# Reordering the last two heads of a decode attention kernel, and filling TensorE's idle times in its tail with unread matmuls

## The chip, the cores and the metric

The kernel runs on one core of a Trainium2 chip. The metric is the device time of one execution in microseconds (us). The span, which the profile and every timed run list beside it, goes from the first to the last instruction; it is mostly 1.8 us shorter than the time. All runs told of here are "fast", which means that none is over 1.5% above the fastest run of the same kernel.

## The reference, cut to what matters

Four sequences decode one token each. The sum of three terms is returned: the input, attention over the last 2048 positions of a cache with 32 heads of 192, and a gated feed-forward block.

```python
xn = _layernorm(x)
q = (xn @ wq)                                   # 4 x 32 heads x 192
k = k_cache[:, :, Sk - W:, :]                   # W = 2048 of 8192 positions
v = v_cache[:, :, Sk - W:, :]
p = _softmax(einsum("bhqd,bhkd->bhqk", q, k) * Dh ** -0.5)
o = einsum("bhqk,bhkd->bhqd", p, v)
return x + o.reshape(B, 1, Hq * Dh) @ wo + (silu(xn @ w1) * (xn @ w3)) @ w2
```

## The kernel before: the parts that matter here

Each head's k block and v block are 3 MB loads. VectorE multiplies k with q in four quarters (`mult`), TensorE sums the products in six matmuls per quarter with an identity as weights (`adder`), VectorE finishes the sums (`reduce_quarter`). Then comes a chain across engines: maximum, transpose, broadcast of the maximum, exponent, and the masked weights `z`. TensorE multiplies them with v (`pv`), a copy and two f32 matmuls add the parts (`ge_sum`), VectorE scales and transposes a group of four heads (`ge_turn`), and TensorE projects it with a block of wo (`ge_proj`). `ffn_out` is the feed-forward block's last projection with w2.

Each engine works through its instructions in the order in which these functions are called. The order comes from a table of slots and phases; the parts for the tail are these:

```python
def pv(h):
    o_ps, z, vt = o_banks[h % 2], zs.pop(h), vts.pop(h)
    for jj in range(NJ // 2):                                  # 32 matmuls of 384 columns
        ...
    nc.scalar.copy(out=o_sb[:], in_=o_ps[:])

ends = {H - 2: (NU - 1, NU), H - 1: (NU + 3, NU + 4)}          # NU = 128 quarters
for h in range(H):
    u0, ul = h * GQ, h * GQ + GQ - 1
    ...
    for u in range(u0, ul + 1):
        add(u, 1, mult, u)
        add(u + 1, 2, adder, u)
        add(u + 1, 8, reduce_quarter, u)
    add(ul + 1, 9, chain_lmax, h)
    add(ul + 2, 3, chain_tr, h)
    add(ul + 2, 4, chain_gmax, h)
    add(ul + 3, 3, chain_bc, h)
    add(ul + 3, 4, chain_z, h)
    add(ul + 4, 5, ge_tot, h)
    ...
    v, m = ends.get(h, (u0 + L, u0 + L + 1))
    add(v, 7, pv, h)
    add(m, 7, ge_sum, h)
...
for h in range(H - 2, H):                                      # all loads of the tail, in this order
    add(NU - 6, 0, load_v, h)
add(NU - 6, 0, w2_load, 0)
add(NU - 6, 0, w2_load, 1)
add(NU - 6, 0, wo_load, NG - 2)
add(NU - 6, 0, wo_load, NG - 1)                                # the last wo block, 983 KB
add(NU - 6, 0, w2_load, 2)
add(NU - 6, 0, w2_load, 3)
add(e - 1, 8, ffn_out, 0)
add(e - 1, 8, ffn_out, 1)
add(e - 1, 8, ge_proj, NG - 2, 0, RPP)
add(e, 6, ge_proj, NG - 1, 0, RPP)                             # the last wo projection
add(e, 7, ffn_out, 2)                                          # with the next line: the last eight matmuls
add(e, 7, ffn_out, 3)
```

## Time and profile before

| | before |
|---|---|
| time, median of three runs | 526.53 us (526.12 to 526.58) |
| profiled span | 523.8 us |
| TensorE busy / VectorE busy | 69% / 65% |
| read from memory | 222.96 MB |

First the page of the kernel before: its rows over 40 equal slices of the span. PE is TensorE, PEld its weight loads, DVE VectorE, ACT ScalarE and POOL GpSimd. PEclk is the granted TensorE clock in tenths, DMA the busy share of the 16 DMA engines in tenths, GB/s what they moved.

```profile
PEclk9979886898878998789997988889878898889988
DMA  9999999999999999999999999999999999999996
GB/s 389 422 443 425 433 431 432 428 433 432 430 435 428 437 418 446 424 437 426 434 434 429 432 434 429 435 427 435 425 437 434 427 437 431 430 434 425 441 418 275
```

The loads never pause until the last slice; the kernel is bound by them, and only the tail behind them is open to this change. The chain that ended last, from its last long waits on, in columns of start, duration and what it was:

```profile
489.68 30.66 DMA w<-in_B_w_dram
520.34 0.04 issue
520.38 0.76 PE acc L264 x8
521.13 0.47 DVE res L542
```

The last w2 load lands at 520.34 us, and only the last eight matmuls, a cast and the output write follow. How close compute was to that shows in the timeline of TensorE in before's tail, with VectorE's transpose of head 31's group (start, duration, engine and line, what it did, and in brackets the idle time ahead of it and what ended it; L340 is `pv`, L264 the projections, L369 the transpose):

```profile
513.30 2.71 PE L340 MATMUL o_ps<-vt,z 128*8 128x384 bf16 x32 [0.24 <-DVE z L332]
...
518.65 0.38 DVE L369 STREAM_TRANSPOSE oT<-og 128x192 bf16<-128x192 bf16 x1
...
519.21 0.98 PE L264 MATMUL acc<-wo_t,oT 128*4 128x320 bf16 x12 [0.47 <-DMA wo_t<-in_A_wo_dram]
...
520.38 0.71 PE L264 MATMUL acc<-w,hT 128*4 128x320 bf16 x8 [0.19 <-DMA w<-in_B_w_dram]
```

Head 31's value product took 2.71 us, mostly at half clock (0.50 from 514 to 516 us). Its transposed output was ready at 519.03 us, 0.2 us ahead of the last wo projection, which waited for its load. The last eight matmuls waited for w2 as well. From the start of that wo projection to the start of the last eight it was 1.17 us; this distance does not shift with the loads.

The stretches of before's tail (the stretch, its length, busy us and instructions of each engine, then the granted clock, the DMA share and GB/s):

```profile
core 0: us, PE busy (x) PEld busy (x) DVE busy (x) ACT busy (x) POOL busy (x), PEclk, DMA share, GB/s
497.00:518.00 21.00, 16.38 (x130) 5.30 (x111) 11.68 (x16) 2.77 (x10) 0.00 (x0) 0.84 0.99 420
518.00:520.30 2.30, 1.72 (x25) 0.87 (x19) 0.80 (x2) 0.00 (x0) 0.00 (x0) 1.00 0.64 256
```

### The profile page before, as it was taken

The numbers are of one execution on the slowest core, as the hardware profiler recorded it, in microseconds if no ns is written. First come the engines' busy times: TensorE is split into PE (matmuls) and PEld (weight loads), VectorE is DVE, ScalarE is ACT, GpSimd is POOL, SyncE is SP. The second block draws the span as 40 slices with busy tenths as digits, with TensorE's granted clock in tenths as the row PEclk, the third lists the DMA queues.
The fourth block names the chain that finished last, engine by engine and source line by source line (L and its number), as shares of the span: only waits on it lengthen the run. The fifth ranks groups of instructions, "written<-read, shape, count | busy, mean of one in ns | idle before, by whom it ended". The sixth has DMA issues, their size and how long they took to land.

```text
span 523.8 us, 4820 instructions
## 1 busy us (share of the span) xinstructions
PE 361.8 (69%) x2336; PEld 75.9 (14%) x1643; DVE 340.9 (65%) x413; ACT 55.8 (11%) x176; POOL 5.6 (1%) x12
## 2 busy tenths in 40 slices
PE   0965866887668776667547768586686876675685
PEld 0100111121111111111111111111111111111122
DVE  3268853687656767577646877466667766667671
ACT  2111111111001110101100111001101110011111
POOL 4000000000000000000000000000000000000000
PEclk9979886898878998789997988889878898889988
DMA  9999999999999999999999999999999999999996
GB/s 389 422 443 425 433 431 432 428 433 432 430 435 428 437 418 446 424 437 426 434 434 429 432 434 429 435 427 435 425 437 434 427 437 431 430 434 425 441 418 275
DMA packets 11904, 223.26 MB, mean 426 GB/s; under 512 B 1332, under 2 KB 1608, under 8 KB 3052
## 3 DMA queue, kind: packets, MB, share of 16 engines
q1 hardware_dynamic: 11868, 222.96, 99.2%
q8 instruction: 15, 0.25, 0.2%
q14 instruction: 5, 0.04, 0.0%
q10 hardware_dynamic: 16, 0.01, 0.0%
HBM read 222.96 MB, written 0.01 MB: 426 GB/s over the span
## 4 chain that ended last, share of the span: by engine, by line
DMA 60%; PE 20%; DVE 15%; ACT 3%; issue 1%; SPq 1%
DMA kt<-in_A_k_cache_dram 44%; PE ps L288 11%; DMA w<-in_B_w_dram 11%; DVE pr L277 10%; DMA vt<-in_A_v_cache_dram 5%; PE po L361 4%; PE qps L243 3%; DVE sc L296 2%; ACT ex L324 1%; DVE z L332 1%; DMA x_sb<-in_A_x_dram 1%; PE mt L318 1%; ACT L324 0%; ACT negm L321 0%; PE mt L305 0%
## 5 line engine op out<-in xcount | busy, mean ns | idle before, releaser
L288 PE MATMUL ps<-pr,idb 128*128 128x512 bf16 x768 | 214.7, 422 | 137.6 <-DVE pr L277 137.5
L277 DVE TENSOR_TENSOR pr<-kt,qbc 128x3072 bf16<-128x3072 bf16 x128 | 223.5, 1746 | 104.0 <-DMA kt<-in_A_k_cache_dram 104.0
L296 DVE TENSOR_REDUCE sc<-ps 128x16 f32<-128x512 f32 x128 | 87.1, 681 | 2.7 <-PE ps L288 2.6
L340 PE MATMUL o_ps<-vt,z 128*8 128x384 bf16 x1024 | 60.5, 380 | 0.2 <-DVE z L332 0.2
L361 PE MATMUL po<-o_sb,sel_w 128*32 128x192 f32 x128 | 49.2, 518 | 0.6 <-ACT o_sb L343 0.6
L340 PEld LDWEIGHTS <-z 128*8 128x8 bf16 x1024 | 26.2, 95 | 98.8 <-issue 89.2
L332 DVE TENSOR_TENSOR z<-ex,mask_b 128x256 bf16<-128x256 bf16 x32 | 13.5, 423 | 38.6 <-ACT ex L324 38.6
L343 ACT COPY o_sb<-o_ps 128x384 f32<-128x384 f32 x32 | 15.3, 478 | 196.9 <-PE o_ps L340 196.9
L313 ACT ACTIVATE gneg<-gmax 1x128 f32<-1x128 f32 x32 | 9.8, 308 | 162.8 <-DVE gmax L310 162.8
L305 PEld LDWEIGHTS mt<-idf,lmax 128*1 128x1 f32 x32 | 3.2, 101 | 127.5 <-issue 125.5
L361 PEld LDWEIGHTS po<-o_sb,sel_w 128*32 128x32 f32 x128 | 13.8, 130 | 29.4 <-issue 27.9
L288 PEld LDWEIGHTS <-idb 128*128 128x128 bf16 x124 | 12.0, 97 | 39.3 <-issue 32.8
L318 PEld LDWEIGHTS mt<-ones_ff,gneg 1*128 1x128 f32 x64 | 9.6, 186 | 47.1 <-issue 43.7
L243 PE MATMUL qps<-wt,xnT 128*128 128x512 bf16 x59 | 14.9, 412 | 0.1
L318 PE MATMUL mt<-ones_ff,gneg 1*128 1x1 f32 x64 | 12.3, 259 | 0.7 <-ACT gneg L313 0.7
L321 ACT COPY negm<-mt 128x1 f32<-128x1 f32 x32 | 5.1, 159 | 70.4 <-PE mt L318 70.4
L310 DVE TENSOR_REDUCE gmax<-mt 1x4 f32<-1x128 f32 x32 | 8.8, 274 | 5.8 <-PE mt L305 5.8
L348 PEld LDWEIGHTS po<-rsum,tot_w 128*32 128x32 f32 x64 | 4.4, 108 | 51.5 <-ACT ex L324 35.4
L249 DVE CAST qbc<-qps 128x512 bf16<-128x512 f32 x6 | 3.8, 684 | 11.7 <-PE qps L243 11.7
L324 ACT ACTIVATE ex<-sc,negm 128x64 bf16<-128x64 f32 x32 | 11.1, 348 | 1.0
L305 PE MATMUL mt<-idf,lmax 128*1 128x128 f32 x32 | 10.9, 340 | 0.0
L199 PE MATMUL xnT_ps<-idb,xn 4*128 4x4 bf16 x5 | 0.4, 178 | 13.4 <-DVE xn L194 13.4
(74 smaller groups left out, 84.4 us busy)
## 6 DMA issues: line engine op xcount, KB each, us to landing
kt<-in_A_k_cache_dram SPq DMA_DIRECT2D x32, 3072.0 KB, 19.1
vt<-in_A_v_cache_dram SPq DMA_DIRECT2D x32, 3072.0 KB, 25.5
wo_t<-in_A_wo_dram SPq DMA_DIRECT2D x8, 960.0 KB, 20.7
wt<-in_A_wq_dram SPq DMA_DIRECT2D x2, 3072.0 KB
w<-in_B_w_dram SPq DMA_DIRECT2D x1, 1920.0 KB
wt<-in_A_wq_dram SPq DMA_DIRECT2D x1, 1536.0 KB, 19.5
w<-in_B_w_dram SPq DMA_DIRECT2D x1, 1536.0 KB
w<-in_B_w_dram SPq DMA_DIRECT2D x2, 640.0 KB
```

What stands on the lines that cost most here:

```text
L243: nc.tensor.matmul(qp[:], lhsT=xnT[:, kc].rearrange("p a b -> p (a b)"), rhs=wq_rows[kc][:, (c0 + i) * QC:(c0 + i + 1) * QC], start=(kc == ...
L277: nc.vector.tensor_tensor(out=pr[:], in0=kts[h][:, g * JQ:(g + 1) * JQ, :], in1=qbc[:, h * Dh:(h + 1) * Dh].unsqueeze(1).to_broadcast([P, ...
L288: nc.tensor.matmul(ps[:], lhsT=idb[:], rhs=pr[:, :, kk * DD:(kk + 1) * DD], start=(kk == 0), stop=(kk == NK - 1))
L296: nc.vector.tensor_reduce(out=scs[h][:, g * JQ:(g + 1) * JQ], in_=pss.pop(u)[:], axis=AX.X, op=ALU.add)
L305: nc.tensor.transpose(out=mt[0:1, 0:P], in_=chs[h][0][:], identity=idf[:])
L313: nc.scalar.activation(out=gneg[:], in_=gmax[:].unsqueeze(1).to_broadcast([1, PB, B]), func=ACTF.Copy, scale=-SCALE)
L318: nc.tensor.matmul(mt[:, P:P + 1], lhsT=gneg[:].rearrange("o p b -> o (p b)"), rhs=ones_ff[:], start=True, stop=True)
L324: nc.scalar.activation(out=ex[:], in_=scs.pop(h)[:], func=ACTF.Exp, bias=negm[:, 0:1], scale=SCALE, accum_out=rsum[:])
L332: nc.vector.tensor_tensor(out=z[:], in0=ex[:].unsqueeze(2).to_broadcast([P, NJ, B]), in1=mask_b[:].unsqueeze(1).to_broadcast([P, NJ, B]), ...
L340: nc.tensor.matmul(o_ps[c * CT:c * CT + 2 * B, :], lhsT=z[:, 2 * jj:2 * jj + 2, :], rhs=vt[:, 2 * jj:2 * jj + 2, :], start=(jj < 4), stop= ...
L343: nc.scalar.copy(out=o_sb[:], in_=o_ps[:])
L361: nc.tensor.matmul(po[sl, 0:Dh], lhsT=sel_w[:, par].rearrange("p a b -> p (a b)"), rhs=o_sb[:, par * Dh:(par + 1) * Dh].rearrange("p (r i) ...
```

## The change

The intent is to shorten the tail behind the last k block. Head 31's last two quarters are multiplied and summed ahead of head 30's value product, so that head 31's softmax can run while head 30's product is done. And 31 matmuls whose result nobody reads are put where TensorE was idle: 16 while the last k block is awaited, 3 and 6 in head 31's softmax chain, 3 ahead of the last wo projection, and 3 behind it. Busy time is meant to keep the clock from being halved. The first part of `ffn_out` also moves ahead of head 31's f32 sum. No load moves.

```diff
+    def warm(n):
+        if "warm" not in ffn:
+            ffn["warm"] = ps_t.tile([P, QC], FP32, tag="t", name="warm")
+        for _ in range(n):
+            nc.tensor.matmul(ffn["warm"][:], lhsT=idb[:], rhs=qbc[:, 0:QC], start=True, stop=True)
+
+    lastu = {NU - 2: (NU - 2, 1, NU - 2, 5), NU - 1: (NU - 2, 2, NU - 2, 6)}
-    ends = {H - 2: (NU - 1, NU), H - 1: (NU + 3, NU + 4)}
+    ends = {H - 2: (NU - 1, NU - 0.4), H - 1: (NU, NU + 1)}
 ...
-            add(u, 1, mult, u)
-            add(u + 1, 2, adder, u)
-            add(u + 1, 8, reduce_quarter, u)
-        add(ul + 1, 9, chain_lmax, h)
 ...
+            ms, mp, as_, ap = lastu.get(u, (u, 1, u + 1, 2))
+            add(ms, mp, mult, u)
+            add(as_, ap, adder, u)
+            add(min(u + 1, NU - 1), 8 if u != NU - 3 else 3, reduce_quarter, u)
+        a, b, c, d = (ul + 1, ul + 2, ul + 3, ul + 4) if h < H - 1 else (NU - 1, NU - 0.5, NU - 0.2, NU)
+        add(a, 9, chain_lmax, h)
 ...
+    add(NU - 3, 1.5, warm, 16)
+    add(NU - 0.3, 0, warm, 3)
+    add(NU - 0.1, 0, warm, 6)
 ...
-    add(e - 1, 8, ffn_out, 0)
+    add(e - 1, 5, ffn_out, 0)
     add(e - 1, 8, ffn_out, 1)
     add(e - 1, 8, ge_proj, NG - 2, 0, RPP)
+    add(e - 1, 9, warm, 3)
     add(e, 6, ge_proj, NG - 1, 0, RPP)
+    add(e, 7, warm, 3)
     add(e, 7, ffn_out, 2)
     add(e, 7, ffn_out, 3)
```

More of the change, by code (lines that the diff above doesn't have):

```diff
@@ L486 @@
         for u in range(u0, ul + 1):
-            add(u, 1, mult, u)
-            add(u + 1, 2, adder, u)
-            add(u + 1, 8, reduce_quarter, u)
-        add(ul + 1, 9, chain_lmax, h)
-        add(ul + 2, 3, chain_tr, h)
-        add(ul + 2, 4, chain_gmax, h)
-        add(ul + 3, 3, chain_bc, h)
-        add(ul + 3, 4, chain_z, h)
-        add(ul + 4, 5, ge_tot, h)
+            ms, mp, as_, ap = lastu.get(u, (u, 1, u + 1, 2))
[4 more added lines that the diff above has]
+        add(a, 9, chain_lmax, h)
+        add(b, 3, chain_tr, h)
+        add(b, 4, chain_gmax, h)
+        add(c, 3, chain_bc, h)
+        add(c, 4, chain_z, h)
+        add(d, 5, ge_tot, h)
         if h % HG == HG - 1:
-            add(ul + 4, 9, ge_rec, h // HG)
+            add(d, 9, ge_rec, h // HG)
         v, m = ends.get(h, (u0 + L, u0 + L + 1))
```

## The prediction

> **What bounds the kernel now.** The loads. The page's DMA row reads 9 in every slice but the last, at 430 GB/s or so. Of the 222.96 MB read, the stretch table gives 432 GB/s from 20 to 497 us and 420 GB/s from 497 to 518 us. The Trainium skill, "DMA: Bandwidth & Descriptors", section "Where 436 GB/s comes from", puts a ceiling at 435 GB/s; this trace sits just under it. TensorE (69% busy) and VectorE (65%) have slack. The chain of waits ends with loads: v until 489.7, then the w2 load until 520.34, then 0.76 us of the last projection's matmuls, 0.47 us of a cast, and the output write to 523.8.
>
> **What the tail looks like.** All loads of the tail are issued by 497.3 us, in an order the change leaves alone. The last k block lands at 497.0. The queue engine's closing waits put the landings of the two wo loads at 516.9 and 519.1 and w2's end at about 520.3. Compute is barely behind: head 31's value product ran 513.30 to 516.01 (2.71 us instead of 1.47, with a granted clock of 0.5 from 514 to 516), its transposed output was ready at 519.03, the last wo projection waited for its load and began at 519.21, ended 520.19, idled 0.19 us for w2, and the last eight matmuls ran 520.38 to 521.09.
>
> **What the change does.** It removes no work. Head 31's last two multiplies (1.75 us each) and sums go ahead of head 30's softmax product; head 31's chain no longer queues behind head 30's value product. It adds 31 unread 512-column matmuls (213 ns each at full clock, estimated from the six-matmul groups' 1.46 us; 6.6 us in all), 28 of them in idle TensorE time, which should hold the clock at 1.0. The Trainium skill, "TensorE: Matmul & The Clock Gate", Part 1, says that an idle window of about 3.4 us halves the clock; this trace agrees (idle 495.2 to 498.8, clock 0.5 from 500).
>
> **What that is worth.** Head 31's product can then start when its v block lands, about 511.5 us (estimate: landing order and 430 GB/s), take 1.5 us, and its transposed output be ready at about 516.5 instead of 519.0. That gain of 2.5 us is off the critical path: the last wo projection still waits for its load at 519.1, and the end for w2 at 520.3. Only about 0.1 us of before's tail waits for compute. Against that, the last three unread matmuls stand between the last wo projection (streaming done at about 520.05) and w2's final matmuls: 0.64 us, of which 0.3 us fits into the wait, so about 0.3 us is lost. In executions where the clock phase left before's end cold, the change could save up to 1 us (20 half-speed 320-column matmuls, in pairs, estimate). These nearly cancel.
>
> **Prediction: 526.5 us, 8 in 10 between 525.5 and 527.2.** Chances: faster by over 2%: 0.01; within 2%: 0.98; slower by over 2%: 0.01.
>
> **What would show it right.** Loads land at the same times after (last w2 at 520.3 within 0.5 us); the granted clock is near 1.0 from 499 to the end; head 31's product starts at v's landing, and its transposed output is ready 2 to 3 us earlier; the last wo projection still starts at its load's landing; no gap for w2 before the last eight matmuls, which start at about 520.7 behind the three unread ones.
>
> **What would make it wrong.** The loads themselves ending earlier or later (contention of TensorE's reads with writes to SBUF); before's unprofiled executions having a cold end, which makes the change about 1 us faster; the 16 unread matmuls running at half clock and pushing head 31's chain past its v block.

## The result, and the profile after

| | before | after |
|---|---|---|
| median of six runs each | 526.33 us (525.66 to 527.12) | 526.79 us (526.04 to 528.43) |
| profiled span | 523.8 us | 524.4 us |
| last wo projection starts | 519.21 us | 519.31 us |
| last eight matmuls start | 520.38 us | 520.98 us |

The ratio is 1.0015, with a 95% interval of 0.9994 to 1.0037: the same within 2%, and not clear of 1. A ratio is the mean time of one kernel's fast runs over that of the other's fast runs of the same rounds, so it is not quite the ratio of the medians.

The same rows of the page, after:

```profile
PEclk9979887989898999798897988789987899889999
DMA  9999999999999999999999999999999999999996
GB/s 387 424 433 428 440 428 428 433 431 431 427 441 429 429 423 443 426 441 427 426 439 427 435 429 433 429 436 429 431 433 429 432 433 432 433 433 431 427 422 264
```

The loads look as before. The chain that ended last, after, from its last long load on:

```profile
484.45 34.82 DMA wo_t<-in_A_wo_dram
519.27 0.04 issue
519.31 0.98 PE acc L264 x12
520.29 0.76 PE warm L484 x3
521.04 0.68 PE acc L264 x8
521.73 0.47 DVE res L558
```

The wo load that lands at 519.27 now ends the waiting, and the three unread matmuls have entered the chain with 0.76 us. TensorE's timeline of after's tail, and the transpose:

```profile
512.16 1.47 PE L484 MATMUL warm<-qbc,idb 128*128 128x512 bf16 x6
...
513.64 1.46 PE L340 MATMUL o_ps<-vt,z 128*8 128x384 bf16 x29
...
517.70 0.38 DVE L369 STREAM_TRANSPOSE oT<-og 128x192 bf16<-128x192 bf16 x1
...
519.31 0.98 PE L264 MATMUL acc<-wo_t,oT 128*4 128x320 bf16 x12 [0.54 <-DMA wo_t<-in_A_wo_dram]
...
520.22 0.82 PE L484 MATMUL warm<-qbc,idb 128*128 128x512 bf16 x3
...
520.98 0.71 PE L264 MATMUL acc<-w,hT 128*4 128x320 bf16 x8
```

Head 31's product now runs at full speed (29 of its 32 matmuls make up this line), and its transposed output is ready at 518.08 us, 0.95 us earlier. That buys nothing, because the last wo projection still starts where its load lands. The distance from its start to that of the last eight has grown from 1.17 to 1.67 us. The stretches of after's tail:

```profile
497.00:518.00 21.00, 19.47 (x157) 5.62 (x119) 12.41 (x18) 2.77 (x10) 0.00 (x0) 1.00 0.99 419
518.00:520.30 2.30, 1.75 (x18) 0.64 (x14) 0.08 (x1) 0.00 (x0) 0.00 (x0) 1.00 0.66 265
```

The clock is 1.00 instead of 0.84 from 497 to 518 us, as intended, while the loads move 419 instead of 420 GB/s.

### The profile page after: what moved, and what is told of

Same layout as the page of the kernel before. It is cut to its first block, busy times and chain, and to the rows that moved or that the text cites. A ratio compares the mean times of both kernels' runs of the same rounds, so it can differ in the third digit from the quotient of the medians.

```text
span 524.4 us, 4855 instructions
## 1 busy us (share of the span) xinstructions
PE 362.1 (69%) x2368; PEld 74.7 (14%) x1646; DVE 341.2 (65%) x413; ACT 55.8 (11%) x176; POOL 5.6 (1%) x12
## 4 chain that ended last, share of the span: by engine, by line
DMA 60%; DVE 20%; PE 16%; ACT 2%; SPq 1%; issue 1%
DMA kt<-in_A_k_cache_dram 48%; DVE pr L277 13%; PE ps L288 8%; DMA wo_t<-in_A_wo_dram 7%; DMA w<-in_B_w_dram 5%; PE po L361 3%; DVE sc L296 3%; PE qps L243 3%; DMA x_sb<-in_A_x_dram 1%; DVE z L332 1%; ACT ex L324 1%; DVE og L366 1%; DVE oT L369 1%; PE mt L318 0%; ACT L324 0%
## 5 line engine op out<-in xcount | busy, mean ns | idle before, releaser
L340 PE MATMUL o_ps<-vt,z 128*8 128x384 bf16 x1024 | 55.1, 353 | 0.0
```

Of the source, the lines that this page charges most:

```text
L340: nc.tensor.matmul(o_ps[c * CT:c * CT + 2 * B, :], lhsT=z[:, 2 * jj:2 * jj + 2, :], rhs=vt[:, 2 * jj:2 * jj + 2, :], start=(jj < 4), stop= ...
```

## The experiments

Twelve kernels ran, in three calls of four, each call on one chip beside 11 runs of the kernel before. Theory A says that the loads set the end, that the reordering and 28 of the unread matmuls lie off the critical path, and that the last three lie on it. The rivals are named in the expectations. There are six fast runs of each kernel, but five of kernels 7 and 12. The medians of before in the three calls were 526.56, 525.81 and 526.24 us.

### 1. Without the last three unread matmuls (e1_no_last3)

```diff
     add(e, 6, ge_proj, NG - 1, 0, RPP)
-    add(e, 7, warm, 3)
     add(e, 7, ffn_out, 2)
```

> The changed kernel without its last three unread matmuls (the only ones behind the last wo projection). Theory A (the loads set the end; only those three lie on the critical path): w2 still lands at about 520.3 us, the last eight matmuls start there at about 520.4 instead of 520.98, and the span is 0.5 to 0.6 us shorter than after's 524.4, equal to before's 523.8 within 0.2. Rival B (the reordering or the other 28 unread matmuls cost the 0.6 us, by slowing the loads): the span stays at 524.2 or above and the wo and w2 landings come later than in before. Rival C (chance of one profile): the last eight matmuls start at no fixed distance behind the w2 landing.

Measured: 526.31 us (525.6 to 527.76), ratio 1.0001 (0.9984 to 1.0018), span 523.8. TensorE's timeline of its end:

```profile
519.10 0.98 PE L264 MATMUL acc<-wo_t,oT 128*4 128x320 bf16 x12 [0.53 <-DMA wo_t<-in_A_wo_dram]
520.26 0.72 PE L264 MATMUL acc<-w,hT 128*4 128x320 bf16 x8 [0.18 <-DMA w<-in_B_w_dram]
```

The distance is 1.16 us again and the last eight wait for w2 again. Rival B falls: with the reordering and 28 unread matmuls still there, the span is before's. Rival C (chance of one profile) falls with the later profiles: the distance is 1.16 or 1.17 us in before and in kernels 1, 2, 7 and 10, which have no unread matmul behind the last wo projection, and 1.66 or 1.67 us in after and in kernels 4 and 12, which have three.

### 2. The reordering alone (e2_reorder_only)

```diff
-    add(NU - 3, 1.5, warm, 16)
-    add(NU - 0.3, 0, warm, 3)
-    add(NU - 0.1, 0, warm, 6)
...
-    add(e - 1, 9, warm, 3)
...
-    add(e, 7, warm, 3)
```

> The reordering alone, no unread matmul at all. Theory A: span as before, 523.8 within 0.3; the last eight matmuls wait for w2 until about 520.4; head 31's product may run at half clock (2.7 us instead of 1.5), its transposed output ready between 517 and 519, without any effect on the end. Rival D (the unread matmuls are what keeps a cold clock off the critical end): the span grows by 0.3 us or more over before, with half-speed 320-column matmuls at the end.

Measured: 525.74 us (525.46 to 526.85), ratio 0.9990 (0.9976 to 1.0004), span 523.9. TensorE's timeline:

```profile
513.10 2.73 PE L340 MATMUL o_ps<-vt,z 128*8 128x384 bf16 x32 [0.24 <-DVE z L332]
...
520.47 0.71 PE L264 MATMUL acc<-w,hT 128*4 128x320 bf16 x8 [0.18 <-DMA w<-in_B_w_dram]
```

As Theory A has it: the product runs at half clock again, and the end still waits for w2. In this order of work, the unread matmuls protect nothing on the critical path (Rival D falls for this kernel).

### 3. Fifteen at the end (e3_last15)

```diff
-    add(e, 7, warm, 3)
+    add(e, 7, warm, 15)
```

> The changed kernel with fifteen instead of three unread matmuls at the end. Theory A: all twelve more, at 213 ns, lie on the critical path: last eight matmuls at about 523.5, span 2.6 us longer than after, about 527.0, time ratio to before about 1.006. Rival B (cost through the loads, not through TensorE's order): the span grows by much less than 2.6 us.

Measured: 529.73 us (528.7 to 530.83), ratio 1.0062 (1.0046 to 1.0078), as expected. The profiled execution was the longest of the six, span 529.0; the spans of the others were 526.9, 526.9, 527.0, 527.1 and 528.4, so four of six lie on the expected 527.0. TensorE's timeline:

```profile
499.63 3.40 PE L484 MATMUL warm<-qbc,idb 128*128 128x512 bf16 x15 [0.16 <-issue]
502.87 0.81 PE L288 MATMUL ps<-pr,idb 128*128 128x512 bf16 x3
...
521.36 0.98 PE L264 MATMUL acc<-wo_t,oT 128*4 128x320 bf16 x12 [0.17 <-DVE oT L369]
522.27 3.41 PE L484 MATMUL warm<-qbc,idb 128*128 128x512 bf16 x15
525.61 0.71 PE L264 MATMUL acc<-w,hT 128*4 128x320 bf16 x8
```

The distance from the wo projection to the last eight is 4.25 us. Twelve more unread matmuls made it 2.58 us longer than after's 1.67, so 215 ns each, all on the critical path.

The first two lines show something not expected. In this execution head 30 had run late and at half clock (0.50 from 486 to 488 and from 496 to 498 us). The 16 unread matmuls (15 records; a few are missing from a trace) then stood in TensorE's order ahead of head 31's first sum. Its product was ready at 499.89 us and its sum began at 502.87. The head's output came at 521.30, and the last wo projection waited for it instead of for its load. This suggested Theory G, tested in 7 and 8. In this execution VectorE could also start on the last k block only at 498.13 us, when it had landed, where in after it started at 497.08; so later loads are a rival cause of such executions, which no run here separates.

### 4. Only the last three, in the kernel before (e4_before_last3)

```diff
 (the kernel before, with warm() added)
     add(e, 6, ge_proj, NG - 1, 0, RPP)
+    add(e, 7, warm, 3)
     add(e, 7, ffn_out, 2)
```

> The kernel before with only the three unread matmuls ahead of w2's last eight, no reordering. Theory A: the last eight start at about 520.9 to 521.0 instead of 520.38, span about 524.4, as in after. Rival B: span as before, 523.8, since the reordering and the other unread matmuls are missing.

Measured: 526.16 us (525.9 to 526.53), ratio 0.9996 (0.9982 to 1.0010), span 524.1. TensorE's timeline:

```profile
519.00 0.98 PE L264 MATMUL acc<-wo_t,oT 128*4 128x320 bf16 x12 [0.56 <-DMA wo_t<-in_A_wo_dram]
...
520.66 0.71 PE L264 MATMUL acc<-w,hT 128*4 128x320 bf16 x8
```

Both numbers are 0.3 us under the expectation, since the loads came 0.2 to 0.3 us earlier than in after. The distance is 1.66 us as in after. So these three alone make the whole of the 0.5 us, without any reordering. The times cannot show it: 0.5 us is 0.1%, inside every interval here. The lowest spans do: 523.7 us in 33 runs of before, 523.7 in kernels 1 and 2, against 524.1 here and 524.2 in 11 runs of after.

### 5 and 6. The last wo load taken away, in both orders (e5_before_cut, e6_after_cut)

```diff
-        oT, wo_t = oTs[hg], wos[hg]
+        oT, wo_t = oTs[hg], wos[min(hg, NG - 2)]
...
-    add(NU - 6, 0, wo_load, NG - 1)
```

The first is the kernel before with this edit, the second is kernel 1 with it. The result is wrong, though the share of one wo block is so small that the comparison with the reference still passed.

> The kernel before without the load of the last wo block (983 KB, 2.2 us of the stream); the last projection uses the block before it, so the result is wrong on purpose. Theory A (before's compute is only just behind the loads): loads end near 518.1 us, but head 31's transposed output is still ready only at about 519.0, so the last projection starts there and the span falls by only 0.3 to 0.6 us, to 523.2 to 523.5. Rival E (before is bound by loads with room to spare): the span falls by the full 2.2 us, to 521.6.

> The same cut (result wrong on purpose) in the changed kernel without its last three unread matmuls. Theory A: head 31's output is ready at about 517.9, the last projection starts at 518.0 to 518.5, span 522.3 to 522.9, so the reordering is worth 0.5 to 1 us once the loads no longer hide it. Rival F (the reordering is worth nothing whatever the loads do): same span as the cut kernel before.

Measured: the first 524.6 us (523.83 to 525.38), ratio 0.9974 (0.9963 to 0.9986), span 523.4; the second 525.14 us (524.87 to 526.55), ratio 0.9988 (0.9975 to 1.0000), span 522.8. The end of the first's timeline of TensorE:

```profile
519.05 0.98 PE L264 MATMUL acc<-wo_t,oT 128*4 128x320 bf16 x12 [0.41 <-DVE oT L369]
519.87 0.71 PE L264 MATMUL acc<-w,hT 128*4 128x320 bf16 x8
```

And that of the second, with the three unread matmuls (two records) that it still has ahead of the last wo projection:

```profile
517.96 0.59 PE L484 MATMUL warm<-qbc,idb 128*128 128x512 bf16 x2 [0.16 <-issue]
518.48 0.98 PE L264 MATMUL acc<-wo_t,oT 128*4 128x320 bf16 x12
519.30 0.71 PE L264 MATMUL acc<-w,hT 128*4 128x320 bf16 x8
```

Taking 2.2 us of loads away from before gains 0.4 us in the profile, as expected: compute was close behind, and now the transposed output is what the wo projection waits for. Over the executions it gains more than expected, though not the 2.2 us of Rival E: the median span of the six is 522.8 us (522.0 to 523.6) against 524.0 for before in this call, so 1.2 us. So the loads bind in before, and compute follows them by 0.4 us in the profiled execution and by about 1.2 us in the median one. Executions in which head 31's product happened to run at full clock would have the larger margin; that is likely, but they were not profiled. The gain of the reordering behind this cut is not shown. One profile against the other it is 0.6 us, but the six spans have medians of 522.8 and 523.05 us, and the times of the changed order are the longer ones (by 0.54 us in the median, half of it outside the span). Rival F is not refuted. Nor is this a clean test of the reordering: in the second profile head 31's output was ready at 517.90 us, and the wo projection began only at 518.48, behind the three unread matmuls.

### 7 and 8. None, and thirty-two, ahead of head 31's first sum (e9_no16, e10_32)

```diff
 (both start from kernel 1)
-    add(NU - 3, 1.5, warm, 16)              # e9_no16: this line removed
+    add(NU - 3, 1.5, warm, 32)              # e10_32: this line instead
```

> The changed kernel without its last three and without the sixteen unread matmuls ahead of head 31's first sum. Theory G (in executions where head 30 ran at half clock, the sixteen stand in TensorE's order between head 31's first product and its sum and push its whole chain, as in the profile of the run with fifteen at the end): profiled span 523.8 to 524.0, and five or six of six times under 526.3, where the kernel without only the last three had three over 526.8. Rival H (those slow times come from the loads, whatever TensorE does): as many times over 526.8 as before has.

> The changed kernel without its last three and with thirty-two instead of sixteen unread matmuls ahead of head 31's first sum. Theory G: sixteen more are 3.4 us, head 31's output comes at about 521.3 instead of 517.9, behind the landing of the last wo block at 519.1, and the span grows by 2.0 to 2.5 us over 523.8; time ratio 1.004 to 1.005. Rival H (that place is off the critical path): span 523.8 to 524.0.

Measured: without them 525.73 us (525.58 to 526.38 in five fast runs), ratio 0.9998 (0.9986 to 1.0010), span 523.9. With thirty-two 526.84 us (526.6 to 530.92), ratio 1.0034 (1.0009 to 1.0060), span 525.2. The timeline of TensorE with thirty-two:

```profile
495.76 6.85 PE L484 MATMUL warm<-qbc,idb 128*128 128x512 bf16 x31 [0.16 <-issue]
502.45 1.46 PE L288 MATMUL ps<-pr,idb 128*128 128x512 bf16 x6
...
520.94 0.98 PE L264 MATMUL acc<-wo_t,oT 128*4 128x320 bf16 x12 [0.17 <-DVE oT L369]
```

So the place of the sixteen has a limited slack: the wo projection waits for head 31 here and starts 1.8 us later than in kernel 1. The span grew by 1.4 us only, less than expected. Head 31's output came at 520.89 instead of 521.3 us, and the last eight, which no longer had to wait for w2, began 0.81 instead of 1.16 us behind the wo projection. The mechanism is shown by this and by the profile in 3. That it makes after's slow executions is not: without the sixteen all times were low (four of five under 526.3 us), but in this call before's were low as well (one of 11 spans above 525.0, against three of 11 in the first call). That part stays open, and kernel 12 speaks against it.

### 9 and 10. A mended order without unread matmuls, cut and whole (e7_mend_cut, e11_mend)

```diff
 (kernel 2, with)
-    ends = {H - 2: (NU - 1, NU - 0.4), H - 1: (NU, NU + 1)}
+    ends = {H - 2: (NU - 1, NU - 0.15), H - 1: (NU, NU + 1)}
```

This puts head 30's f32 sum behind head 31's broadcast. The first of the two has the cut of 5 and 6 as well and is wrong.

> The reordering with no unread matmul, head 30's sum moved behind head 31's broadcast in TensorE's order, and the last wo load cut as in the two kernels before it (result wrong on purpose). Theory I (head 31's product came at 513.4 and not at its v block's landing because head 30's sum and nine unread matmuls stood in the order ahead of it): the product now starts at 511.5 to 512.0, head 31's output is ready by 516.5 to 517.5, the last eight matmuls end near 519.0, span 521.6 to 522.2. Rival J (the product waits for its v block, landing at about 513): it still starts at 513.0 or later, span 522.5 or more.

> The same order without the cut, a correct kernel. Theory A: the gain of 1 to 2 us in head 31's output buys nothing, since the last wo projection still starts at its load's landing at 519.1 and the last eight matmuls at w2's at 520.3; span 523.7 to 524.1, ratio to before 0.998 to 1.001. Rival K (the ends of before's executions often wait for compute): the ratio is under 0.998.

Measured: the whole one 525.65 us (525.54 to 527.46), ratio 0.9995 (0.9979 to 1.0011), span 523.9. Its timeline of TensorE:

```profile
511.64 1.47 PE L340 MATMUL o_ps<-vt,z 128*8 128x384 bf16 x32
...
519.24 0.98 PE L264 MATMUL acc<-wo_t,oT 128*4 128x320 bf16 x12 [1.31 <-DMA wo_t<-in_A_wo_dram]
520.41 0.72 PE L264 MATMUL acc<-w,hT 128*4 128x320 bf16 x8 [0.18 <-DMA w<-in_B_w_dram]
```

Head 31's product starts 1.9 us earlier than in after, so Theory I holds and the v block was not what it waited for (Rival J falls). The output is ready at 516.11 us, nearly 3 us ahead of before's 519.03, and the time does not move: the plainest sign that this chain is off the critical path. Rival K asks for a ratio under 0.998, and it was 0.9995; the interval just reaches that.

The cut one: 524.53 us (523.95 to 525.5), ratio 0.9966 (0.9952 to 0.9981), span 523.6. It misses the expected 521.6 to 522.2, though the product started at 511.42. Its stretches show where the time went (columns as above):

```profile
516.00:517.00 1.00, 0.15 (x4) 0.10 (x5) 0.00 (x0) 0.00 (x0) 0.00 (x0) 1.00 0.65 265
517.00:518.00 1.00, 1.00 (x12) 0.55 (x10) 0.00 (x0) 0.00 (x0) 0.00 (x0) 0.58 0.53 204
518.00:519.00 1.00, 1.00 (x12) 0.47 (x10) 0.00 (x0) 0.00 (x0) 0.00 (x0) 0.50 0.01 1
```

TensorE had so little left to do that it idled 1.59 us for the next wo load, and the clock was halved when the last projections ran: 24 of their matmuls took 3.10 us, where two groups of 12 take 0.98 us each at full clock. That the idle time halved the clock is argued, not shown: kernel 10 has the same gap of 1.59 us and then one of 1.31, and its clock stayed at 1.00 to the end. Kernel 9's six spans fall into two sets, 522.1 to 522.3 and 523.1 to 523.7 us. That the lower set is the one with a full clock at the end is likely, but was not profiled.

### 11. Fewer matmuls behind the last landing (e8_mend_split)

```diff
 (kernel 10, with)
     add(NU - 6, 0, w2_load, 1)
+    add(NU - 6, 0, w2_load, 2)
+    add(NU - 6, 0, w2_load, 3)
     add(NU - 6, 0, wo_load, NG - 2)
     add(NU - 6, 0, wo_load, NG - 1)              # now as two loads, of 4 and 2 of its 6 parts
-    add(NU - 6, 0, w2_load, 2)
-    add(NU - 6, 0, w2_load, 3)
...
+    add(e - 1, 7.5, ffn_out, 2)
+    add(e - 1, 7.5, ffn_out, 3)
     add(e, 6, ge_proj, NG - 1, 0, RPP)
-    add(e, 7, ffn_out, 2)
-    add(e, 7, ffn_out, 3)
```

> The same order, with all of w2 loaded ahead of the wo blocks and the last wo block in two loads, so that four instead of eight matmuls follow the last landing. Theory A: the last landing stays at 520.2 to 520.4, the last matmuls take 0.47 instead of 0.71 us, span 523.5 to 523.7, ratio 0.998 to 1.000, hardly to be told from 1. If the loads' order or the extra split costs something, the landing is later and the span above 524.

Measured: 526.54 us (526.22 to 527.98), ratio 1.0007 (0.9992 to 1.0023), span 524.5, a miss. The end of its timeline of TensorE:

```profile
518.57 0.98 PE L267 MATMUL acc<-wo_t,oT 128*4 128x320 bf16 x12 [1.42 <-DMA wo_t<-in_A_wo_dram]
520.17 1.49 PE L267 MATMUL acc<-wo_t,oT 128*4 128x320 bf16 x12 [0.62 <-DMA wo_t<-in_A_wo_dram]
```

Two things went wrong. The first part of the last wo block itself landed only at 520.13 us, about when w2, the last of before's loads, lands there, so all twelve matmuls, not four, came behind that. The second part was issued only at 504.3 us; in before all loads of the tail are issued by 497.3. And the clock was halved for the last of them (0.77 from 520 to 521 us, 0.50 from 521 to 522), so they took 1.49 instead of 0.98 us.

### 12. The changed kernel once more (e12_after_again)

No edit.

> The changed kernel once more, beside the others on one chip. Theory A: ratio to before 1.001 (0.5 us), the last eight matmuls at 520.9 to 521.0 in an undisturbed profile. Theory G (the sixteen unread ones push head 31's chain when head 30 ran at half clock): one or more of six times at 527.3 or above, more often than in the kernels without them. Rival H: no more slow times than before has.

Measured: 526.15 us (526.1 to 527.05 in five fast runs), ratio 0.9998 (0.9984 to 1.0011), span 524.3. The 0.5 us of Theory A lies within the interval. The profile repeats it: the last wo projection begins at 519.24 us, where its load lands, and the last eight at 520.90, 1.66 us behind it. No time reached 527.3, so Theory G's share in the slow executions is not confirmed: over all calls, seven of before's 33 spans are above 525.0 us, and four of after's 11, too few to tell them apart.

No correct version beat before. The best times, those of kernels 2, 7 and 10, have ratios whose intervals hold 1, and ends that wait for w2 like before's.

## Why the prediction was right or wrong

- **The range and the class were right.** 526.79 us lies in 525.5 to 527.2, and the change was called the same within 2%.
- **The bound was right.** The last wo projection and w2 wait for their loads in before and in kernels 1, 2, 7 (without the sixteen) and 10. Making head 31's output almost 3 us earlier (10) changed nothing. That compute is only just behind the loads holds for the profiled executions (kernel 5 gained 0.4 of 2.2 us in its profile), but less for the others (1.2 us in the median).
- **The clock was right.** It was predicted near 1.0 from 499 us on, and it was 1.00 from 497 to 518 us.
- **"Its transposed output be ready at about 516.5" was wrong.** It was 518.08 us. The product was to start when its v block landed, but head 30's f32 sum (1.52 us) and the nine unread matmuls of the chain stood ahead of its steps in TensorE's order. In after's timeline the three held head 31's broadcast back by 0.75 us and the six its product by 0.2 us; most of the rest of the 1.9 us falls to the sum. With these out of the way (10) the product started at 511.64 us, close to the estimate of 511.5. The statement that 28 of the 31 unread matmuls lie in idle time failed with it: the nine delayed the chain, and the sixteen do so when head 30 is late (3). It cost no time only because the chain had slack.
- **"About 0.3 us is lost" was too small.** The distance from the last wo projection to the last eight matmuls grew from 1.17 to 1.67 us, so 0.50 us. The prediction had the three begin 0.84 us behind the projection's start and last 0.64 us; they began 0.91 us behind it and held the last eight back for 0.76 us.
- **"In executions where the clock phase left before's end cold, the change could save up to 1 us" was not seen.** In before's profile and in kernel 2's the end ran at full clock, and the lowest spans with and without the first 28 unread matmuls agree. A cold end was seen only in kernels 9 and 11, whose compute is done early, and not in kernel 10, where it is too; so what brings it about stays open. Before's slower executions were not profiled. So the two terms said to nearly cancel did not: one was 0.5 us, and of the other nothing shows.
- **That the number was so near is in part luck.** The range also holds the medians of before and those of eight of the nine correct kernels tried here, so falling into it tells little about the terms inside the sum.

## What to carry to other kernels

Before speeding up a chain, look at what the step behind its end waits for; here that was a load, and up to 3 us less compute were worth nothing. A filler instruction is free only if nothing behind it in its engine's order can be ready before it is done, in a late execution too; the three placed between the last two needed pieces of work cost their full length less the wait that was there. Conversely, work that is made to end early leaves idle time in which the clock can fall (it did in kernels 9 and 11, not in 10), so check the granted clock of the stage that is left on the critical path.

## What the Trainium skill lacked or had wrong

- "TensorE: Matmul & The Clock Gate", Part 1: its rule against idle gaps above some 3.4 us does not settle these cases. In before the clock fell to 0.5 at 513 to 514 us after gaps that since 499 us were at most 0.72 us, with TensorE busy 0.57 us of the 2 from 511 to 513. In kernel 9 it fell at 517 us after a longest gap of 1.59 us, with TensorE busy 2.26 us of the 3 from 513 to 516. In kernel 10 it stayed at 1.00 after the same gap and a further one of 1.31 us, with TensorE busy 1.35 us of the 4 from 515 to 519. The same Part does tell of one kernel whose clock went up and down with many short idle times; no run here shows what decides.
- The same page says that weight loads are pulled ahead of running matmuls, under conditions, and gives the time of one load, but not what a group of full 128-column weights between groups of 4-column weights costs: three matmuls of 215 ns took 0.76 us of the chain instead of 0.64, and fifteen (kernel 3) 3.34 instead of 3.22. So each group cost some 0.12 us more; of what this consists was not tested.
- "DMA: Bandwidth & Descriptors", "Where 436 GB/s comes from", says that some 358 GB/s bind for loads from memory, next to a measurement of its own of 425; with one core streaming, 432 GB/s were measured here from 20 to 497 us, just under the page's other ceiling of 435. So the 358 did not bind here.
- No page says how the end of a long stream of loads looks: over its last 2.3 us the rate fell to 256 to 265 GB/s at a DMA share of 0.64 to 0.66, and in kernel 11 the first of the two loads issued last landed at 520.13 us, hardly before the last load of the kernel before (520.34).
